# One activation on a column of ones, ahead of all other work on ScalarE

## The chip, the cores and the metric

The kernel runs on one NeuronCore of one Trainium2 chip. The time is that of one launch on the device in microseconds (us), and what counts is the median over several launches. The compute engines are TensorE (PE in the rows; PEld is its loading of weights), VectorE (DVE), ScalarE (ACT) and GpSimd (POOL). Most transfers are issued by the queue of the sync engine (SP). Each engine takes its own instructions in their written order and waits for the others through semaphores.

## The reference, cut to what matters

An attention with normalized queries and keys is followed by two feed-forward layers:

```
q_n, k_n = rmsnorm(q, g_q), rmsnorm(k, g_k)        # 4 batches, 12 heads, 448 rows, 64 columns, float32
attn = softmax(q_n @ k_n.T / sqrt(64)) @ v
x = attn, heads side by side                        # 1792 x 768
h = x @ w_in;  x = (h * sigmoid(1.702 * h)) @ w_out # 768 -> 2048 -> 768
h = x @ w_in2; out = (max(h, 0) + alpha * min(h, 0)) @ w_out2
```

## The kernel before

The work goes in pairs of heads. For each pair a tile `qk` (128 partitions, 2 x 7 x 64 float32) takes the rows of k and q by four transfers, and ScalarE squares it in two halves (function `normalize`, line 421, `sq<-qk`). VectorE adds up each half over 64 columns (line 423, `ss<-sq`), and GpSimd turns the sums of both halves into reciprocal roots by three rounds of Newton's method (lines 424 to 434, `ss`, `rs`, `tn`). VectorE then scales the rows (line 458, `qn<-qk,rs`), TensorE transposes them (lines 465 and 467, `qt`), and ScalarE copies the result out and multiplies it by a column of the gains (line 468, scale `g_col`). From there on scores, softmax and the product with v follow for each pair, while the weights of the first feed-forward layer are loaded and split into high and low halves (`w1i`, `w1o`). The three other batches of the attention run beside the first layer on TensorE, and the second layer is last: a product with `w2i`, a store of its result `g_dram`, and an output product (line 1090) whose operands `w2lo`, `w2hi`, `even` and `odd` are sums and differences of blocks.

The order on each engine is fixed when the program is built: a scheduler goes through the code and lays out one list of instructions for each engine. At the front of the program the code reads:

```
if True:
    make_identity(nc, ident)
    nc.vector.memset(ones, 1.0)
    nc.vector.tensor_copy(out=identf, in_=ident)
    load_qk(0)
    gains()
...
    next(w1i_steps)
    normalize(0)
```

`load_qk(0)` puts four transfers on the queue of SP (lines 378 to 381). `gains()` puts two more behind them, for `gq` and `gk`, the two gain vectors (lines 282 and 283); VectorE multiplies them (line 284, `gq<-gq,gk`) and makes the scaled tile `gs` from them (line 293), TensorE transposes it (line 296, `gt`), and ScalarE writes `g_col` (line 297). ScalarE has a table of functions that an instruction of its own, ACT_TABLE_LOAD, loads; no line of the code asks for it, the build puts it ahead of the first activation. In the whole program there is one, and all activations use the same table.

Of the kernel before, what the change touches and what calls it, by code (L numbers as in the profile page):

```python
# [9 lines left out]
F32 = mybir.dt.float32  # L10
# [3 lines left out]
AF = mybir.ActivationFunctionType  # L14
# [43 lines left out]
def attention_moe_kernel(  # L58
# [17 lines left out]
    nc = tc.nc  # L76
# [14 lines left out]
    small = ctx.enter_context(tc.tile_pool(name="small", bufs=2))  # L91
# [7 lines left out]
    ones = const.tile([128, 128], BF16, name="ones")  # L99
# [155 lines left out]
    def later_rows(w, d, other):  # L255

        nj = w.shape[1]
        return lambda j: w[:, j + d].rearrange("p e n -> p (e n)").bitcast(F32) if j + d < nj else other(j)
# [20 lines left out]
    def gains():  # L279
        gq = small.tile([128, D], F32, tag="gq", name="gq", bufs=1)  # L280
        gk = small.tile([128, D], F32, tag="gk", name="gk", bufs=1)
        nc.sync.dma_start(out=gq, in_=g_q.partition_broadcast(128))
        nc.sync.dma_start(out=gk, in_=g_k.partition_broadcast(128))
        nc.vector.tensor_tensor(out=gq, in0=gq, in1=gk, op=ALU.mult)
        gm = small.tile([128, 1], F32, tag="gm", name="gm", bufs=1)
        gi = small.tile([128, 1], F32, tag="gi", name="gi", bufs=1)
        nc.vector.tensor_reduce(out=gm, in_=gq, op=ALU.max, axis=AX, apply_absolute_value=True)
        pow2floor(c_s, gm)
        scaled_reciprocal(gi, c_s, 0.5)
        nc.vector.memset(gs[64:128, 3], 1.0)  # L290
        for c in range(4):
            ps = slice(0, 64 if c == 3 else 128)
            nc.vector.tensor_scalar(out=gs[ps, c], in0=gq[ps], scalar1=gi[ps], scalar2=None, op0=ALU.mult)
        nc.vector.tensor_scalar(out=c_s, in0=c_s, scalar1=2.0 ** -22, scalar2=None, op0=ALU.mult)
        gt = ps_m.tile([128, 128], F32, tag="m", name="gt")
        nc.tensor.transpose(out=gt, in_=gs[:, 0:2].rearrange("p c d -> p (c d)"), identity=identf)
        nc.scalar.activation(out=g_col, in_=gt[:, 0:1], func=AF.Copy, scale=c_s)

    def v_scales(b, col):
        one = small.tile([128, 1], F32, tag="vone", name="vone")  # L300
        nc.vector.tensor_reduce(out=one, in_=col, op=ALU.max, axis=AX)
        pow2floor(one, one)
        partition_max(mv[:, b:b + 1], one)
        scaled_reciprocal(av[:, b:b + 1], mv[:, b:b + 1], 2.0 ** 13)
# [65 lines left out]
    def load_qk(P):  # L370

        if P >= B * NP:
            return
        b, p = divmod(P, NP)
        qk = raw_p.tile([128, 2, NT2, D], F32, tag="qk", name="qk", bufs=QKB)
        places = qk.rearrange("p h c d -> p h (c d)")
        queue = loader(P)
        queue.dma_start(out=places[:, :, 0:3 * D], in_=main_rows(k, b, p))
        queue.dma_start(out=places[:, :, 4 * D:], in_=main_rows(q, b, p))
        queue.dma_start(out=qk[0:64, :, 3], in_=some_rows(k, b, p, ST))  # L380
        queue.dma_start(out=qk[64:128, :, 3], in_=some_rows(q, b, p, ST))
        raws[P] = qk

    def load_v(P):
        if P >= B * NP:
            return
        b, p = divmod(P, NP)
        if b:
            vr = raw_p.tile([128, 2, NV, D], F32, tag="vr", name="vr")
        else:  # L390
            firsts[P] = first_tiles(P)
            vr = firsts[P][1]
        queue = loader(P)
        queue.dma_start(out=vr.rearrange("p h c d -> p h (c d)")[:, :, 0:3 * D], in_=main_rows(v, b, p))
        h = 0 if b else 64
        queue.dma_start(out=vr[h:h + 64, :, 3], in_=some_rows(v, b, p, ST))
        queue.dma_start(out=vr[64 - h:128 - h, :, 3], in_=some_rows(v, b, p, 0, 3))
        rawv[P] = vr
# [783 lines left out]
    if True:  # L1182
        make_identity(nc, ident)
        nc.vector.memset(ones, 1.0)
        nc.vector.tensor_copy(out=identf, in_=ident)
        load_qk(0)
        gains()
        load_v(0)
        load_qk(1)
        load_v(1)  # L1190
        g0 = big.tile([128, KF, 2, S], F16, tag="g", name="g0")
        stage = g0.rearrange("p m e t -> p (m e t)").bitcast(F32)
        parts = stage[:, 0:R1I * 1024].bitcast(I32).rearrange("p (i n t) -> p i n t", i=R1I, t=2)
        raw1o = g0.rearrange("p m e t -> p m (e t)").bitcast(I32)[:, KF - 4 * R1O:, FIRST:].rearrange("p m (n t) -> p m n t", t=2)

        def num1i(j):
            if j == KD - 1:
                return stage[:, 5120:5120 + FF]
            return held.bitcast(F32)[:, (j - 3) * FF:(j - 2) * FF]

        def num1o(j):
            if j == KF - 2:
                return att_p.tile([128, 2 * NT2 * D], F32, tag="ph", name="num1o", bufs=PHB)[:, 0:DM]
            return raw_p.tile([128, 2 * NT2 * D], F32, tag="qk", name="num1o", bufs=QKB)[:, 0:DM]

        w1i_steps = weights(
            moe_w_in, "w1i", lambda: w1i, later_rows(w1i, 3, num1i), lambda t: parts[:, t % R1I], 4, R1I, 2.0 ** -14, scales,
            G1I
        )
        w1o_steps = weights(  # L1210
            moe_w_out, "w1o", lambda: w1o, later_rows(w1o, 2, num1o), lambda t: raw1o[:, 4 * (t % R1O):4 * (t % R1O) + 4], 2,
            R1O, 2.0 ** -25, scales, G1O
        )
        next(w1i_steps)
        normalize(0)
        for _ in prep_pair(0):
            pass
        for P in range(2, 1 + QKB):
            load_qk(P)
        load_v(2)  # L1220
        normalize(1)
        early = measure(1, B - 1, 4)
        for i, _ in enumerate(first_pairs()):
            if i >= 6:
                for _ in range(1):
                    next(early, None)
            for _ in range(W_RATE):
                next(w1i_steps, None)
        for _ in w1i_steps:
            pass  # L1230
        v_scales(0, v0)
        first_x()
        moe1_scales(0)
        for P in range(NP, NP + 2):
            load_qk(P)
            load_v(P)
        n1o = 0
        steps = attention([4 * P + r for P in range(NP) for r in range(2, 4)])
        for i, _ in enumerate(steps):
            pairs = max(0, (i - LAG + 1) // 2)  # L1240
            rows = KF - 2 if pairs >= 4 else (HOLD + pairs * HELD) // (2 * DM) - 2
            while n1o < min(1 + 2 * rows + 3 * (rows // 2), (i + 1) * W1O_RATE, 57):
                next(w1o_steps)
                n1o += 1
            if i >= M_AT and i - M_AT < KF:
                first_in(slice(0, FIRST), i - M_AT, g0)
            for _ in range(2):
                next(early, None)
        while n1o < 57:
            next(w1o_steps)  # L1250
            n1o += 1
        for m in range(len(range(2 * NP + LAG)) - M_AT, KF):
            first_in(slice(0, FIRST), m, g0)
        with tc.issue_after(loads["w1o"][W1O_HOLD].ins):
            normalize(NP, NP + 1)
            for _ in prep_pair(NP):
                pass
            load_qk(NP + 2)
            load_qk(NP + 3)
            load_v(NP + 2)  # L1260
        att_steps = other_batches()
        done = 4 * NP
        late = late_weights(ctx, att)
        for b in range(B):
            last = min(NU, 4 * NP * (b + 2)) + LAG2
            first = done
            got = None
            for i, _ in enumerate(moe1(b) if b else first_moe1(g0)):
                lead = 0 if b else B1_AT
                want = first + (last - first) * min(1.0, max(0.0, i + 1 - lead) / (PACE[b] * TICKS - lead))  # L1270
                while done < min(want, NU + LAG2):
                    next(att_steps)
                    done += 1
                if b == B - 1:
                    for _ in range(1 if i < 2 * KF else 2):
                        if got is None or i >= 2 * KF:
                            got = next(late, None)
        second_layer(late)
# [30 lines left out]
```

## Time and profile before

| what | us |
|---|---|
| median of 3 runs | 1150.96 |
| lowest and highest run | 1147.56, 1157.47 |
| time of the profiled execution | 1150.36 |
| its span, from the first to the last instruction | 1148.6 |

The profile is of one execution. Its time is 1.76 us more than its span. In that execution TensorE worked in 93% of the span and ScalarE in 60%, and TensorE's granted clock was 0.977 of full speed in the mean.

### The profile page before, as it was taken

The numbers are of one execution on the slowest core, as the hardware profiler recorded it, in microseconds if no ns is written. First come the engines' busy times: TensorE is split into PE (matmuls) and PEld (weight loads), VectorE is DVE, ScalarE is ACT, GpSimd is POOL, SyncE is SP. The second block draws the span as 40 slices with busy tenths as digits, with TensorE's granted clock in tenths as the row PEclk, the third lists the DMA queues.
The fourth block names the chain that finished last, engine by engine and source line by source line (L and its number), as shares of the span: only waits on it lengthen the run. The fifth ranks groups of instructions, "written<-read, shape, count | busy, mean of one in ns | idle before, by whom it ended". The sixth has DMA issues, their size and how long they took to land.

```text
span 1148.6 us, 18408 instructions
## 1 busy us (share of the span) xinstructions
PE 1069.4 (93%) x6753; PEld 585.0 (51%) x6753; DVE 802.1 (70%) x1397; ACT 693.2 (60%) x1452; POOL 179.4 (16%) x364
## 2 busy tenths in 40 slices
PE   4776889898989999999999999999999999999998
PEld 2343457744444445555455455444444477666664
DVE  5979798887879885577534865599976224959341
ACT  4778686888879876688633562356456425756120
POOL 2701003676433342100000000000000000000000
PEclk9978899899999999999999999999999999999999
DMA  7974743478888756455446501765351423363111
GB/s 227 258 178 132 182 129 109 97 158 184 183 191 167 160 130 151 109 121 118 78 124 229 203 1 64 249 215 194 136 171 59 138 70 113 106 184 101 33 31 28
DMA packets 235562, 158.19 MB, mean 138 GB/s; under 512 B 167888, under 2 KB 214736, under 8 KB 235472
## 3 DMA queue, kind: packets, MB, share of 16 engines
q1 hardware_dynamic: 229200, 141.34, 44.6%
q0 software_dynamic: 6272, 15.67, 5.3%
q8 instruction: 53, 0.87, 0.3%
q14 instruction: 37, 0.30, 0.1%
HBM read 92.35 MB, written 25.69 MB: 103 GB/s over the span
## 4 chain that ended last, share of the span: by engine, by line
PE 56%; DVE 16%; DMA 11%; issue 7%; ACT 6%; POOL 4%; SPq 1%; DVEq 0%; POOLq 0%; ACTq 0%
PE op L1090 17%; PE yp L821 15%; PE h L927 9%; PE hp L798 7%; PE xp L648 3%; PE sp L525 2%; DMA t<-hl 2%; PE hp L758 2%; DMA g<-in_moe_w_in_dram 2%; DVE nm L530 1%; DMA g<-in_moe_w_out_dram 1%; DVE g L141 1%; ACT pr L550 1%; DMA qk<-in_q_dram 1%; DMA yr<-y_dram 1%
## 5 line engine op out<-in xcount | busy, mean ns | idle before, releaser
L821 PE MATMUL yp<-g,w1o 128*128 128x448 f16 x1152 | 226.9, 354 | 1.5 <-DVE g L767 0.9
L927 PE MATMUL h<-x,w2i 128*128 128x512 f16 (+1 forms) x1152 | 219.3, 352 | 4.3 <-DVE pos L933 2.8
L798 PE MATMUL hp<-x,w1i 128*128 128x448 f16 x864 | 170.3, 353 | 1.6 <-DVE t L807 1.6
L927 PEld LDWEIGHTS <-w2i 128*128 128x128 f16 x1152 | 112.6, 98 | 109.6 <-issue 5.1
L821 PEld LDWEIGHTS <-w1o 128*128 128x128 f16 x1152 | 109.5, 98 | 110.8 <-issue 12.0
L798 PEld LDWEIGHTS <-w1i 128*128 128x128 f16 x864 | 81.9, 98 | 83.5 <-issue 9.6
L620 DVE SCALAR_TENSOR_TENSOR ph<-pr,sm,ph 128x448 f16<-128x448 f32 x126 | 85.2, 707 | 25.4 <-ACT ph L593 25.4
L530 DVE TENSOR_REDUCE nm<-sp 128x2 f32<-128x896 f32 x96 | 92.5, 964 | 10.3 <-PE sp L525 7.6
L932 ACT ACTIVATE pos<-h,sign 128x512 f32<-128x512 f32 (+1 forms) x64 | 40.1, 628 | 89.7 <-PE h L927 83.3
L550 ACT ACTIVATE pr<-sp,nm,c_s 128x448 f32<-128x448 f32 x126 | 89.9, 717 | 2.4 <-DVE ph L620 1.1
L1090 PEld LDWEIGHTS <-even 128*128 128x128 f16 x672 | 65.7, 98 | 43.5
L933 DVE SCALAR_TENSOR_TENSOR pos<-h,slope,pos 128x512 f32<-128x512 f32 (+1 forms) x64 | 43.4, 680 | 59.9 <-ACT pos L932 59.7
L593 ACT ACTIVATE ph<-pr,sm 128x448 f16<-128x448 f32 x126 | 77.6, 659 | 10.7 <-DVE sm L590 10.6
L758 PE MATMUL hp<-x,w1i 128*128 128x256 f16 (+1 forms) x576 | 66.1, 276 | 9.2 <-DVE g L767 5.2
L1090 PEld LDWEIGHTS <-odd 128*128 128x128 f16 x504 | 49.3, 98 | 32.6
L758 PEld LDWEIGHTS <-w1i 128*128 128x128 f16 x576 | 55.2, 104 | 20.2 <-issue 14.8
L1090 PE MATMUL op<-w2lo,even 128*128 128x384 f16 x384 | 63.5, 326 | 0.0
L648 PE MATMUL xp<-pt,vs 128*64 128x256 f16 (+1 forms) x792 | 49.8, 267 | 7.5 <-DMA pt<-ph 6.2
L525 PE MATMUL sp<-t 64*128 64x448 f16 (+1 forms) x432 | 54.0, 357 | 0.6 <-DMA t<-hl 0.5
L648 PEld LDWEIGHTS <-vs 128*64 128x64 f16 x792 | 37.9, 112 | 27.6 <-issue 17.2
L532 ACT ACTIVATE nm<-nm,c_s 128x2 f32<-128x2 f32 x72 | 20.9, 290 | 48.5 <-DVE nm L530 48.1
L1090 PE MATMUL op<-w2hi,even 128*128 128x384 f16 x288 | 47.5, 326 | 0.0
(243 smaller groups left out, 1659.7 us busy)
## 6 DMA issues: line engine op xcount, KB each, us to landing
g<-in_moe_w_in_dram SPq DMA_DIRECT2D x24, 512.0 KB, 6.1
g<-in_moe_w_out_dram SPq DMA_DIRECT2D x32, 384.0 KB, 4.0
w2raw<-in_moe_w_in_dram SPq DMA_DIRECT2D x24, 512.0 KB, 5.7
w2raw<-in_moe_w_out_dram SPq DMA_DIRECT2D x16, 768.0 KB, 6.4
g_dram<-pos SPq DMA_DIRECT2D x48, 256.0 KB, 2.0
gp<-g_dram SPq DMA_DIRECT2D x8, 1024.0 KB, 6.8
odd<-g_dram SPq DMA_DIRECT2D x6, 1024.0 KB, 5.5
y_dram<-y SPq DMA_DIRECT2D x24, 224.0 KB, 2.5
```

The costliest lines, as they stand in the source:

```text
L525: nc.tensor.matmul(out=sp[:, j, 0:S] if n == 2 else sp[ds, 0, 0:S], lhsT=qt[ds] if n == 2 else qt[ds, 64:128], rhs=kt[ds, 0:S], start=(i = ...
L530: nc.vector.tensor_reduce(out=nm[:, 0:n], in_=sp[:, 0:n, 0:S], op=ALU.max, axis=AX, negate=True)
L550: last = nc.scalar.activation(out=pr[i], in_=sp[:, i, 0:S], func=AF.Exp, bias=nm[:, i:i + 1], scale=c_s if u >= 4 * NP else 1.0, accum_out ...
L593: nc.scalar.activation(out=ph[:, i, 0:S], in_=pr[i], func=AF.Copy, scale=sm[:, i:i + 1])
L620: nc.vector.scalar_tensor_tensor(out=ph[:, i, S:2 * S], in0=pr[i], scalar=sm[:, i:i + 1], in1=ph[:, i, 0:S], op0=ALU.mult, op1=ALU.subtract)
L648: nc.tensor.matmul(out=xp[64 * j:64 * j + 64, t:t + n], lhsT=vs[ks, j, c], rhs=pt[ks, 7 * j + kc, 0:n] if b else pt[ks, kc, o:o + n], star ...
L758: nc.tensor.matmul(out=ps, lhsT=w1i[:, kk, e, m * 128:(m + 1) * 128], rhs=xs[0, kk][:, f, cols], start=(i == 0), stop=(i == 3 * KD - 1))
L798: nc.tensor.matmul(out=ps, lhsT=w1i[:, kk, e, m * 128:(m + 1) * 128], rhs=x[:, f], start=(n == 0), stop=(n == 3 * KD - 1))
L821: nc.tensor.matmul(out=ps, lhsT=w1o[:, m, e, j * 128:(j + 1) * 128], rhs=g[:, m, f], start=(n == 0), stop=(n == 3 * KF - 1))
L927: nc.tensor.matmul(out=ps, lhsT=w2i[:, kk, e, m * 128:(m + 1) * 128], rhs=x2[kk][:, f], start=(c == 0), stop=(c == 3 * KD - 1))
L933: nc.vector.scalar_tensor_tensor(out=pos, in0=ps, scalar=slope[:, m:m + 1], in1=pos, op0=ALU.mult, op1=ALU.max)
L1090: nc.tensor.matmul(out=ps, lhsT=ops[:, o, m, f], rhs=rhs[:, e], start=(c == 0), stop=(c == 3 * KH - 1))
```

## The change

One tile `first` of one column is taken from the pool `small`, and one activation writes the square of a column of ones into it. Nothing reads the tile.

```
@@ -1182,6 +1182,8 @@
     if True:
         make_identity(nc, ident)
         nc.vector.memset(ones, 1.0)
+        first = small.tile([128, 1], F32, tag="first", name="first", bufs=1)
+        nc.scalar.activation(out=first, in_=ones[:, 0:1], func=AF.Square)
         nc.vector.tensor_copy(out=identf, in_=ident)
         load_qk(0)
         gains()
```

On ScalarE, at the very front of the program, the load of the table had stood ahead of the first square and had waited with it for the transfers of `qk`. DMAHW0 to DMAHW7 are the semaphores of SP's transfers, in turn, and the numbers behind semaphores and buffers mean nothing here:

```order
-L1304 UNCONDITIONAL_BRANCH [waits barrier_Pool_Activation_PE_DVE_SP_release]
-L421 ACT_TABLE_LOAD [waits DMAHW2_49,DMAHW3_49,DMAHW1_49]
-L421 ACTIVATE sq<-qk 128x448 [waits DMAHW0_49]
+L1306 UNCONDITIONAL_BRANCH [waits barrier_Pool_Activation_PE_DVE_SP_release]
+L1186 ACT_TABLE_LOAD
+L1186 ACTIVATE first<-ones 128x1 [waits DVE_49]
+L421 ACTIVATE sq<-qk 128x448 [waits DMAHW2_49,DMAHW3_49,DMAHW1_49,DMAHW0_49]
 L421 ACTIVATE sq<-qk 128x448
 L297 ACTIVATE g_col<-gt,c_s 128x1 [waits PE_49]
```

The load now waits for nothing but the barrier at the start, the new activation waits for VectorE's memset of `ones`, and the first square waits for its four transfers by itself. On VectorE, at the same place, the list is as it was but for line numbers; DMAHW4 and DMAHW5 are the transfers of `gq` and `gk`:

```order
-L1304 UNCONDITIONAL_BRANCH [waits barrier_Pool_Activation_PE_DVE_SP_release]
+L1306 UNCONDITIONAL_BRANCH [waits barrier_Pool_Activation_PE_DVE_SP_release]
 L1184 MEMSET ones 128x128
 L290 MEMSET gs 64x64
-L1185 CAST identf<-ident 128x128 [waits Pool_49]
+L1187 CAST identf<-ident 128x128 [waits Pool_49]
 L423 TENSOR_REDUCE ss<-sq 128x7 [waits Activation_49]
 L284 TENSOR_TENSOR gq<-gq,gk 128x64 [waits DMAHW5_49,DMAHW4_49]
```

Nothing moved there: the product of the gains stands between the sum of the first half (the row above it) and the sum of the second half (the next row of the list, `L423` again). The lists of TensorE, GpSimd and SP are the same as before too, and all later rows of ScalarE and VectorE.

The new tile takes 4 bytes of each partition, for which the build sets aside 32. Every tile behind it in the on-chip memory therefore starts 32 bytes further on: 993 of the 1107 tiles, among them `qk`, `sq`, `hl`, `t`, `pt`, `vs`, `gp`, `w2hi`, `y` and `pos`. The large buffers for weights, `g`, `odd`, `even` and the second layer's `w2lo` keep their places. Before, nearly all the large moved tiles started at a multiple of 64 bytes, and now they start 32 past one; the unmoved ones start 32 past a multiple of 64 in both programs.

## Rows read from the trace of the kernel before

**Rows 1.** The page: engines' busy time; the chain that ended last, by engine and line.

```profile
PE 1069.4 (93%) x6753; PEld 585.0 (51%) x6753; DVE 802.1 (70%) x1397; ACT 693.2 (60%) x1452; POOL 179.4 (16%) x364
...
PE 56%; DVE 16%; DMA 11%; issue 7%; ACT 6%; POOL 4%; SPq 1%; DVEq 0%; POOLq 0%; ACTq 0%
PE op L1090 17%; PE yp L821 15%; PE h L927 9%; PE hp L798 7%; PE xp L648 3%; PE sp L525 2%; DMA t<-hl 2%; PE hp L758 2%; DMA g<-in_moe_w_in_dram 2%; DVE nm L530 1%; DMA g<-in_moe_w_out_dram 1%; DVE g L141 1%; ACT pr L550 1%; DMA qk<-in_q_dram 1%; DMA yr<-y_dram 1%
```

**Rows 2.** Timeline of ScalarE: start, length, instruction [idle before, what ended it].

```profile
4.79 1.28 ACT L421 ACT_TABLE_LOAD   x1 [4.79 <-DMA qk<-in_q_dram]
6.09 1.04 ACT L421 ACTIVATE sq<-qk 128x448 f32<-128x448 f32 x2
11.81 0.26 ACT L297 ACTIVATE g_col<-gt,c_s 128x1 f32<-128x1 f32 x1 [4.68 <-PE gt L296]
```

**Rows 3.** Timeline of VectorE, the first 10 us.

```profile
0.83 0.17 DVE L1184 MEMSET ones<- 128x128 bf16 x1 [0.83 <-PEq L1293]
...
6.70 0.62 DVE L423 TENSOR_REDUCE ss<-sq 128x7 f32<-128x448 f32 x1 [5.13 <-ACT sq L421]
8.60 0.23 DVE L284 TENSOR_TENSOR gq<-gq,gk 128x64 f32<-128x64 f32 x1 [1.28 <-DMA gk<-in_g_k_dram]
8.74 0.61 DVE L423 TENSOR_REDUCE ss<-sq 128x7 f32<-128x448 f32 x1
```

**Rows 4.** The chain that ended last, in order of time: start, length, link.

```profile
2.55 0.61 SPq L381
...
3.21 0.59 SPq L282
...
3.84 4.65 DMA gk<-in_g_k_dram
...
8.60 0.23 DVE gq L284
8.82 0.54 DVE ss L423
...
9.45 0.27 POOL ss L424
...
13.34 0.23 POOL rs L434
...
13.59 0.07 DVE qn L458
```

**Rows 5.** Groups of instructions, shapes apart: count, busy us, mean ns, idle before.

```profile
L1090 PE MATMUL op<-w2lo,even 128*128 128x384 f16 x384 | 63.5, 326 | 0.0
L1090 PE MATMUL op<-w2hi,even 128*128 128x384 f16 x288 | 47.5, 326 | 0.0
...
L1030 ACT ACTIVATE gp<-gp,cg 128x256 f32<-128x256 f32 x64 | 26.4, 494 | 12.8 <-DMA gp<-g_dram 8.3 <-DVE cg L1163 4.5
...
L1030 ACT ACTIVATE odd<-odd,cg 128x256 f32<-128x256 f32 x48 | 19.7, 496 | 10.9 <-DMA odd<-g_dram 10.9
...
L165 DVE SCALAR_TENSOR_TENSOR w2n<-w2raw,w2n 128x512 int32<-128x512 int32 x24 | 15.8, 685 | 0.1
...
L165 DVE SCALAR_TENSOR_TENSOR w1i<-g,w1i 128x512 int32<-128x512 int32 x12 | 8.1, 684 | 0.1
```

**Rows 6.** DMA issues by line: count, KB each, median us from issue to landing.

```profile
g<-in_moe_w_in_dram SPq DMA_DIRECT2D x24, 512.0 KB, 6.1
...
w2raw<-in_moe_w_in_dram SPq DMA_DIRECT2D x24, 512.0 KB, 5.7
...
gp<-g_dram SPq DMA_DIRECT2D x8, 1024.0 KB, 6.8
odd<-g_dram SPq DMA_DIRECT2D x6, 1024.0 KB, 5.5
y_dram<-y SPq DMA_DIRECT2D x24, 224.0 KB, 2.5
```

**Rows 7.** All transfers into the tile `gp`.

```profile
DMA to landing us min/median/max: 5.1/6.8/9.1
```

**Rows 8.** All transfers into the tile `odd`.

```profile
DMA to landing us min/median/max: 5.2/5.5/7.8
```

More of the change, by code (lines that the diff above doesn't have):

```diff
@@ L1184, in attention_moe_kernel @@
         nc.vector.memset(ones, 1.0)
+        first = small.tile([128, 1], F32, tag="first", name="first", bufs=1)
+        nc.scalar.activation(out=first, in_=ones[:, 0:1], func=AF.Square)
         nc.vector.tensor_copy(out=identf, in_=ident)
```

## The prediction

> **What bounds the kernel now.** I read the page first. Its chain that ended last is 56% TensorE, and ScalarE holds 6% of it, DMA 11% [rows 1]. TensorE is busy in 93% of the span and ScalarE in 60%, so an instruction on ScalarE is worth its length only where nothing else is late beside it. The instruction that moves lies in the first 14 us, and there TensorE's share says nothing: the stretch is one chain of small steps, and the question is which step is last at each join. So the next views are the timelines of ScalarE and VectorE, and then the chain in order of time.
>
> On ScalarE the table load starts at 4.79 us, when the last transfer of `qk` that it waits for has landed, and takes 1.28 us [rows 2]. The two squares start 0.02 us behind it and end at 6.09 + 1.04 = 7.13 us. The first of them releases VectorE's sum at 6.70 [rows 3], and on that view alone the load seems to cost 1.28 us: VectorE sat idle 5.13 us until then. But the next row of VectorE is the product of the gains, which waited another 1.28 us for the transfer of `gk` and began at 8.60. (That the load and this wait are both 1.28 us long is chance.) The sum of the second half stands behind that product and began at 8.74, 1.61 us after its own input was ready at 7.13. GpSimd needs both sums, and started at 9.45 [rows 4].
>
> The chain in order of time says the same from the other side. It begins with SP's issues, goes into the transfer of `gk` (issued at 3.84, 4.65 us long), and from its landing into the gains at 8.60, the second sum at 8.82, GpSimd at 9.45 to 13.57 and the scaling of the rows at 13.59 [rows 4]. Neither the load nor the squares are links of it. The start of this kernel is bound by the sixth transfer in SP's queue.
>
> **The change part by part.** *The load leaves its place.* The first square can start where the load started, at 4.79, and both end at 4.79 + 1.04 = 5.83 us instead of 7.13. The first sum then starts about 6.70 - 1.30 = 5.40 and ends at 6.02. Behind it VectorE meets the product of the gains, as before, and the order of VectorE and SP is unchanged, so the transfer of `gk` is issued and lands when it did. The wait there grows from 1.28 to 8.60 - 6.02 = 2.58 us. The second sum starts at 8.74 as before. What is late next is thus not a new thing but the one that was late already: the saving of 1.30 us is turned into wait on VectorE. The two squares of the second pair cannot use it either, since the copy to `g_col` at 11.81 stands ahead of them on ScalarE [rows 2], and it hangs on the gains too. On the path: 0.
>
> *The load at its new place.* It waits only for the barrier at the start, behind which VectorE's first instruction ran at 0.83 [rows 3]. I take the same for ScalarE: an estimate of 0.83 to 2.11 us, in a stretch where ScalarE did nothing for 4.79 us. The cover is 2.7 us up to the landing of `qk` at 4.79, and from there another 2.8, since the two squares are late for the gains only if they start after 8.60 - 1.04 = 7.56. Without the cover it would cost its 1.28 us, which it did not even at its old place. So 0.
>
> *The new activation.* The nearest row is the other activation of one column, `g_col`, 0.26 us [rows 2]. Its input, the memset of `ones`, ends at 0.83 + 0.17 = 1.00, before the load ends, so it waits for nothing of its own: about 2.11 to 2.4 us, under the same cover. Queued behind it on ScalarE is only the first square, which waits for `qk` to 4.79. Nobody waits for `first`. Cost 0; without cover 0.26.
>
> *The 32 bytes.* Every tile behind the new one starts 32 bytes later. For the compute engines the trace before has both alignments side by side, since `w2lo` sat 32 past a multiple of 64 and `w2hi` on one: 326 ns for a matmul with either [rows 5]. ScalarE took 494 ns on `gp` (on a multiple) and 496 on `odd` (32 past one), VectorE 685 and 684 for the same operation on `w2n` and `w1i`. So 0 for the engines. For transfers the rows are further off, because load differs between stages: `odd`, 32 past, landed in 5.5 us in the median against 6.8 for `gp`; `g`, 32 past, in 6.1 against 5.7 for `w2raw` [rows 6]. The two pairs have opposite signs, and the least disturbed transfers of the first pair differ by 0.1 us, 5.1 against 5.2 [rows 7, 8]. I take 0 and keep, for the range, 0.1 / 5.1 = 2% either way, and 6.1 / 5.7 = 7% as an upper bound; I leave out the 1.3 us by which the median of `odd` is better, because the minimum shows none of it. On the chain DMA has 11%, of which 3% are the loads of `g`, which does not move [rows 1]: 8% of 1148.6 = 92 us. So -1.8 to +6.4 us, and 0 taken.
>
> The sum is 0 + 0 + 0 + 0: the profiled execution's 1150.36 us stays. The median of the runs shown is 0.6 us above it, with runs from 1147.56 to 1157.47, so the forecast for the median is **1151.0 us**. A difference of under 1%, 11.5 us, is about what a measurement of this kernel cannot tell from no change.
>
> **The rivals.** *A: the load was on the path.* Then 1.28 us come off, 1151.0 - 1.3 = 1149.7 us. For it speaks that ScalarE and VectorE both stood still for the load; against it the second sum, which was ready 1.61 us before it ran, and the chain, which goes through `gk`. It would take a `gk` that lands 1.6 us earlier than in this trace before the squares count at all, and 2.9 us earlier for the whole price. By the Trainium skill, page "ScalarE: Activation LUTs", section "What ACT_TABLE_LOAD costs", a load takes about 1283 ns and a drain of about 1380 ns with it, 2.66 us in all; by that this rival would give an estimated 1148.3 us. The trace agrees with the 1283 ns and shows no drain: the square starts 0.02 us behind the load [rows 2]. Here the engine had nothing in flight to drain.
>
> *B: the shift slows the transfers.* This is the case on the slower side. The transfers of `hl` to `t`, of `ph` to `pt`, of `y`, of `gp` and of `qk` all read or write moved tiles, and they make 8% of the chain. At 2% more they cost 1.8 us, at 7% more 6.4 us: 1152.8 to 1157.4 us. It would be over 1% only where these transfers got 11.5 / 92 = 12.5% longer. Against it stand the equal minima of `gp` and `odd` [rows 7, 8]; for it, that the transposes have no row at the other alignment, so nothing here excludes that they mind. The Trainium skill says in "DMA: Bandwidth & Descriptors", section "How a descriptor splits into AXI transactions", that a transfer is cut at multiples of 256 bytes of address and that a descriptor which does not start on one also fetches the bytes from the boundary down to its start, in beats of 32 bytes. That speaks against this change: a row of `y` of 1792 bytes went from 128 past such a boundary to 160 past it, 60 beats to 61, an estimated 1.7% more. By that the 92 us would grow by an estimated 1.6 us. No run so far shows it; the minima of `gp` and `odd` neither exclude nor need it.
>
> *C: the change doesn't do what it says.* The load could take longer at the front than at its old place, or be repeated. The order has one load, at the front, so the second is out. For the first, the load may last up to 7.56 - 0.26 - 0.83 = 6.5 us, five times its 1.28, before the gains wait for a square; past that the time grows one for one: at ten times its length it would be 12.8 - 6.5 = 6.3 us, 1157.3.
>
> **How the numbers follow.** The forecast, no change beyond the scatter of the runs, has 0.74. A has 0.08, B 0.14, C 0.02, and 0.02 are left for what I don't see. The range goes down to the lowest run shown less the 1.8 us by which transfers may get better, 1145.8, and up to 1157.5, which is the upper end of B and the highest run shown alike. The forecast, A, most of B and C lie in it; what is left out is the far end of B and a median of the new runs outside the runs of before, together some 2 in 10. Faster by over 1% would need 11 us that no row offers: 0.02. Slower by over 1% is B beyond 12.5%: 0.04. The rest, 0.94, is within 1%.
>
> **What would show it.** In the changed kernel's trace the load should begin near 0.8 us and last 1.28, the activation on `ones` follow it at 0.3 us or less, and the first square begin near 4.8. The first sum on VectorE should come at about 5.4 with some 3.8 us idle before it, and the product of the gains at about 8.6 with 2.6 us idle before it instead of 1.28, still released by `gk`. The second sum, GpSimd's first step (9.45) and the row scaling (13.59) should stand within some 0.2 us of where they stood. The matmul groups should keep 326 ns, and the medians of `gp` and `y` their 6.8 and 2.5 us. I am wrong in the start if the second sum runs by the squares and not by the gains, and wrong in the rest if the transfers on moved tiles, the transposes above all, land later by more than a few per cent while those into `g` do not.

## The result, and the profile after

The changed kernel takes 1158.77 us in the median of 22 runs (1151.67 to 1165.62), the kernel before 1150.57 us in 22 runs. The ratio is 1.0068, with a 95% interval of 1.005 to 1.0087: slower by 7.8 us (5.8 to 10.0) on 1150.57; the two medians lie 8.2 us apart. It was forecast unchanged, at 1151.0 us. Ratios and intervals in this document leave out three single executions far off all others: 1393.27 us of the kernel before, 2178.43 us of the shift by 128 bytes, and 2755.26 us of the kernel with only the transposes' sources moved, which was its profiled one.

The page of the changed kernel, engines and the chain that ended last, against [rows 1]:

```profile
PE 1069.4 (92%) x6753; PEld 583.9 (50%) x6753; DVE 804.7 (69%) x1397; ACT 693.6 (60%) x1453; POOL 181.6 (16%) x364
...
PE 52%; DMA 15%; DVE 14%; issue 7%; ACT 6%; POOL 4%; SPq 1%; DVEq 0%; ACTq 0%; POOLq 0%
```

TensorE and ScalarE have the same work to the microsecond, VectorE and GpSimd 2.6 and 2.2 us more, and the span is 10.1 us longer, 1158.7 after 1148.6. The chain says where to look: DMA's share of it went from 11% to 15%, and TensorE's fell.

The front of the program is the first place to check. The timeline of ScalarE, against [rows 2]:

```profile
0.72 1.28 ACT L1186 ACT_TABLE_LOAD   x1 [0.72 <-PEq L1295]
2.02 0.20 ACT L1186 ACTIVATE first<-ones 128x1 f32<-128x1 bf16 x1
4.76 1.04 ACT L421 ACTIVATE sq<-qk 128x448 f32<-128x448 f32 x2 [2.54 <-DMA qk<-in_q_dram]
12.18 0.26 ACT L297 ACTIVATE g_col<-gt,c_s 128x1 f32<-128x1 f32 x1 [6.38 <-PE gt L296]
```

And that of VectorE, against [rows 3]:

```profile
0.82 0.17 DVE L1184 MEMSET ones<- 128x128 bf16 x1 [0.82 <-PEq L1295]
...
5.37 0.62 DVE L423 TENSOR_REDUCE ss<-sq 128x7 f32<-128x448 f32 x1 [3.81 <-ACT sq L421]
8.97 0.23 DVE L284 TENSOR_TENSOR gq<-gq,gk 128x64 f32<-128x64 f32 x1 [2.98 <-DMA gk<-in_g_k_dram]
9.11 0.61 DVE L423 TENSOR_REDUCE ss<-sq 128x7 f32<-128x448 f32 x1
```

The load runs at 0.72 us with nothing beside it, and the squares start 1.33 us earlier than before. All of that is turned into wait for `gk`: VectorE idles 2.98 us for it, where it had idled 1.28. The second sum follows the gains by 0.14 us, as before. In this execution `gk` landed 0.37 us later, so even this stretch ends later, but 0.4 us is not 10.

So where are the 10 us? The products of the attention with v (line 648, operands `pt` and `vs`) run through the three later batches and nowhere else; each row of the view by line gives the first and the last start. Before:

```profile
L648 PE MATMUL xp<-pt,vs x792: 246/272/370, 239.7 to 614.1; 128*64 128x256 f16 x108, 128*64 128x192 f16 x90
```

After:

```profile
L648 PE MATMUL xp<-pt,vs x792: 246/272/422, 240.5 to 625.7; 128*64 128x256 f16 x108, 128*64 128x192 f16 x90
```

The first product is 0.8 us late, the last 11.6. Behind it nothing more is lost; the first matmul of the second layer starts at 740.7 us instead of 729.5, 11.2 later, and the span ends 10.1 later. In this pair of executions the whole loss lies in the attention of the three later batches, which is the part with transposes by DMA. The view by stretches, from the first start of these products to the last (length; busy time and count of PE, PEld, DVE, ACT, POOL; TensorE's granted clock; DMA share; GB/s), before:

```profile
239.70:614.10 374.40, 365.65 (x2588) 183.81 (x2587) 257.10 (x436) 278.93 (x667) 106.41 (x202) 0.99 0.64 142
```

After:

```profile
240.50:625.70 385.20, 369.75 (x2588) 185.01 (x2587) 257.90 (x434) 278.14 (x663) 107.94 (x202) 0.98 0.71 138
```

Of the 10.8 us more, 6.7 are idle time of TensorE (15.45 us instead of 8.75), and 4.1 are longer busy time for the same 2588 matmuls, at a granted clock of 0.98 of full speed in the mean instead of 0.99. The DMA engines are busy in 71% of it instead of 64%. The largest wait of TensorE there is the one for `pt`, which the transposes write (us, times, longest), before:

```profile
PE xp L648 <- DMA pt<-ph: 6.2, 3, 3.2
```

After:

```profile
PE xp L648 <- DMA pt<-ph: 13.8, 5, 6.2
```

Operands that moved do not slow the engines, as the page's groups from the second layer show, against [rows 5]:

```profile
L1090 PE MATMUL op<-w2lo,even 128*128 128x384 f16 x384 | 63.5, 326 | 0.0
L1090 PE MATMUL op<-w2hi,even 128*128 128x384 f16 x288 | 47.5, 326 | 0.0
...
L1030 ACT ACTIVATE gp<-gp,cg 128x256 f32<-128x256 f32 x64 | 26.3, 495 | 11.9 <-DMA gp<-g_dram 8.4 <-DVE cg L1163 3.5
```

`w2hi` and `gp` moved by 32 bytes, and take 326 and 495 ns where they took 326 and 494. Some transfers do not keep their time. The issues in the changed kernel (count, KB each, median us to landing), the first four with rows of before in [rows 6]:

```profile
g<-in_moe_w_in_dram SPq DMA_DIRECT2D x24, 512.0 KB, 5.9
...
gp<-g_dram SPq DMA_DIRECT2D x8, 1024.0 KB, 6.8
odd<-g_dram SPq DMA_DIRECT2D x6, 1024.0 KB, 5.4
...
y_dram<-y SPq DMA_DIRECT2D x24, 224.0 KB, 2.4
...
vr<-in_v_dram POOLq DMA_DIRECT2D x16, 192.0 KB, 3.7
...
vs<-vs SPq DMA_DIRECT2D x36, 48.0 KB, 2.8
pt<-ph SPq DMA_TRANSPOSE x90, 4.1
...
t<-hl SPq DMA_TRANSPOSE x18, 4.4
```

The same view before, of the last four, for which the prediction gave no row:

```profile
vr<-in_v_dram POOLq DMA_DIRECT2D x16, 192.0 KB, 3.2
...
vs<-vs SPq DMA_DIRECT2D x36, 48.0 KB, 2.3
...
pt<-ph SPq DMA_TRANSPOSE x90, 3.6
...
t<-hl SPq DMA_TRANSPOSE x18, 3.7
```

The transposes take 19% (into `t`) and 14% (into `pt`) longer in the median, and the copies inside `vs` and the loads into `vr`, which run beside them, 22% and 16%. `gp` and `y`, moved as well, are as fast as before. The transposes into `pt` are of two sizes. The 54 that read 128 x 1792 numbers (line 627) and the 36 that read 64 x 896, a quarter of that (line 632), took before:

```profile
DMA to landing us min/median/max: 3.4/3.6/7.1
DMA to landing us min/median/max: 2.4/3.4/5.1
```

And after:

```profile
DMA to landing us min/median/max: 4.0/4.3/9.1
DMA to landing us min/median/max: 2.6/3.6/8.7
```

The large ones lose 0.6 us at their shortest, the small ones 0.2. The page's row of SP's transfers shows the same in sum, before:

```profile
q1 hardware_dynamic: 229200, 141.34, 44.6%
```

And after:

```profile
q1 hardware_dynamic: 229200, 141.34, 47.0%
```

Packets and megabytes are equal, but they held each of the 16 DMA engines for 47.0% of 1158.7 = 545 us instead of 44.6% of 1148.6 = 512. The single packets in the two traces tell whose time this is. The 149,504 packets of 256 bytes on this queue, of which the transposes make up an estimated 145,152 by the shapes of what they read, held each engine for 217.9 us instead of 186.1, and all its other packets for 326.2 instead of 326.6. So the added time is that of the transposes; the copies beside them land later, but hold the engines no longer.

### The profile page after: what moved, and what is told of

The parts are those of the page before. It is cut to its first block, busy times and chain, and to the rows that moved or that the text cites. A ratio compares the mean times of both kernels' runs of the same rounds, so it can differ in the third digit from the quotient of the medians.

```text
span 1158.7 us, 18409 instructions
## 1 busy us (share of the span) xinstructions
PE 1069.4 (92%) x6753; PEld 583.9 (50%) x6753; DVE 804.7 (69%) x1397; ACT 693.6 (60%) x1453; POOL 181.6 (16%) x364
## 4 chain that ended last, share of the span: by engine, by line
PE 52%; DMA 15%; DVE 14%; issue 7%; ACT 6%; POOL 4%; SPq 1%; DVEq 0%; ACTq 0%; POOLq 0%
PE op L1090 16%; PE yp L821 14%; PE h L927 9%; PE hp L798 7%; DMA qk<-in_q_dram 4%; PE xp L648 3%; DMA g<-in_moe_w_out_dram 2%; DMA g<-in_moe_w_in_dram 2%; PE sp L525 2%; ACT pr L550 1%; DMA pt<-ph 1%; DMA t<-hl 1%; DMA yr<-y_dram 1%; DVE g L141 1%; DVE w2num L165 1%
## 5 line engine op out<-in xcount | busy, mean ns | idle before, releaser
L821 PE MATMUL yp<-g,w1o 128*128 128x448 f16 x1152 | 229.4, 356 | 1.1 <-ACT g L140 0.7
L620 DVE SCALAR_TENSOR_TENSOR ph<-pr,sm,ph 128x448 f16<-128x448 f32 x126 | 87.7, 727 | 23.6 <-ACT ph L593 23.5
L593 ACT ACTIVATE ph<-pr,sm 128x448 f16<-128x448 f32 x126 | 77.6, 659 | 11.6 <-DVE sm L590 10.9
L758 PE MATMUL hp<-x,w1i 128*128 128x256 f16 (+1 forms) x576 | 63.3, 269 | 10.0 <-DVE g L767 6.3
```

Of the source, the lines that this page charges most:

```text
L593: nc.scalar.activation(out=ph[:, i, 0:S], in_=pr[i], func=AF.Copy, scale=sm[:, i:i + 1])
L620: nc.vector.scalar_tensor_tensor(out=ph[:, i, S:2 * S], in0=pr[i], scalar=sm[:, i:i + 1], in1=ph[:, i, 0:S], op0=ALU.mult, op1=ALU.subtract)
L758: nc.tensor.matmul(out=ps, lhsT=w1i[:, kk, e, m * 128:(m + 1) * 128], rhs=xs[0, kk][:, f, cols], start=(i == 0), stop=(i == 3 * KD - 1))
L821: nc.tensor.matmul(out=ps, lhsT=w1o[:, m, e, j * 128:(j + 1) * 128], rhs=g[:, m, f], start=(n == 0), stop=(n == 3 * KF - 1))
```

## The experiments

Theory 1: the shift by 32 bytes slows transfers on moved tiles. Theory 2, the rival: something of the load or the activation at the front costs. Five kernels tell them apart, two with one part of the change each and three with another size of the shift. Each ratio here is of 7 to 12 runs against 28 or 35 of the kernel before.

**The tile alone.** VectorE sets it, and the load stays where it was.

```
+        first = small.tile([128, 1], F32, tag="first", name="first", bufs=1)
+        nc.vector.memset(first, 1.0)
```

> The kernel before with the tile alone: first is taken from the pool, so that everything behind it moves by 32 bytes, and VectorE sets it instead of ScalarE; the table's load stays in front of the first square. Theory 1, the shift of 32 bytes slows the transfers on moved tiles: as slow as the changed kernel, 1.005 to 1.009 of before, transposes into t in the median near 4.4 us (3.7 before) and into pt near 4.1 (3.6). Theory 2, the load and the activation at the front are what costs: 1.000 within 0.002, transposes at 3.7 and 3.6.

Measured: 1.0063 (1.0041 to 1.0086), transposes into `t` at 4.5 us and into `pt` at 4.1. The tile alone, with no activation in front, gives the loss of the whole change within the intervals.

**The activation alone.** It writes into `g_col`, which the build has anyway.

```
+        nc.scalar.activation(out=g_col, in_=ones[:, 0:1], func=AF.Square)
```

> The activation on a column of ones stands in front, but writes into g_col, which is overwritten later, so that no tile moves. Theory 1 (the shift): 1.000 within 0.002 of before, with the first square at 4.8 us and the gains still the late step at 8.6 to 9.0. Theory 2 (the front): 1.005 to 1.009.

Measured: 0.9993 (0.9971 to 1.0015), transposes at 3.7 and 3.7. Theory 2 is out, and the load at the front is worth nothing that can be measured. The interval alone would still have room for the 1.3 us of rival A of the prediction (0.9989), but VectorE's timeline has not: the first sum comes 1.21 us earlier than before, `gk` landed early in this execution, and still the second sum follows the gains:

```profile
5.49 0.62 DVE L423 TENSOR_REDUCE ss<-sq 128x7 f32<-128x448 f32 x1 [3.94 <-ACT sq L421]
8.13 0.23 DVE L284 TENSOR_TENSOR gq<-gq,gk 128x64 f32<-128x64 f32 x1 [2.02 <-DMA gk<-in_g_k_dram]
8.28 0.61 DVE L423 TENSOR_REDUCE ss<-sq 128x7 f32<-128x448 f32 x1
```

**Other sizes of the shift.** The change, with a wider tile (16, 32 and 64 columns):

```
-        first = small.tile([128, 1], F32, tag="first", name="first", bufs=1)
-        nc.scalar.activation(out=first, in_=ones[:, 0:1], func=AF.Square)
+        first = small.tile([128, 16], F32, tag="first", name="first", bufs=1)
+        nc.scalar.activation(out=first[:, 0:1], in_=ones[:, 0:1], func=AF.Square)
```

By 64 bytes:

> The change with first made 64 bytes wide: all that the change moves is moved by 64 bytes. Theory 1 in the form that what counts is a start at a multiple of 64 bytes: 1.000 within 0.002 of before, transposes at 3.7 and 3.6 us. Theory 1 in the form of cuts at multiples of 256 bytes, by which any start off such a boundary costs: the tiles hl, t, pt and vs now start 64 past one, so transposes stay at 4.1 to 4.4 us and the time at 1.005 or more. Theory 2 (the front): 1.005 to 1.009.

By 256 bytes:

> The change with first made 256 bytes wide: every moved tile keeps its place with respect to boundaries of 256 bytes and of all smaller powers of two. Theory 1 in either form: 1.000 within 0.002 of before, transposes at 3.7 and 3.6 us. Theory 2 (the front): 1.005 to 1.009.

By 128 bytes:

> The change with first made 128 bytes wide, so that all moved tiles move by 128 bytes: hl, t, pt, vs and vr now start 128 past a multiple of 256, and qk, y, pos, gp, yr and ob, which had started 128 past one, on one. Boundaries of 256 count: transposes at 4.1 to 4.4 us, copies inside vs near 2.8, the loads of qk by GpSimd no longer than before (3.9) or shorter, the time 1.002 to 1.007. Boundaries of 128 count: transposes at 3.7 and 3.6, 1.000 within 0.002.

Measured: 64 bytes 1.0051 (1.0028 to 1.0073), 128 bytes 1.0038 (1.0011 to 1.0066), 256 bytes 0.9996 (0.9974 to 1.0017). A shift that keeps the place against multiples of 256 costs nothing, all others cost. The transfers that read `hl` are the clearest sign: their shortest is 3.4 us in every profile with `hl` on a multiple of 256 and 4.0 in every one with it off. The view by tile gave 3.4/3.7/6.6 us (shortest, median, longest) before. At 64 bytes:

```profile
DMA to landing us min/median/max: 4.0/4.5/6.4
```

At 128 bytes:

```profile
DMA to landing us min/median/max: 4.0/4.4/6.3
```

At 256 bytes:

```profile
DMA to landing us min/median/max: 3.4/3.7/6.7
```

At 32 bytes, in the changed kernel, it was 4.0/4.4/6.4. The step is the same 0.6 us for 32, 64 and 128, and a packet of 256 bytes took 23.3, 23.2 and 23.5 ns in the mean, 19.9 before. The shift by 128 also put `qk` on a multiple of 256, and GpSimd's loads of q did not get shorter for it (4.0 us, 3.9 before).

Next: which of the moved tiles is it? Pads in front of single tiles move them alone. The helper is the same in the four kernels that follow; each names its pads in bytes.

```
+    class Padded:
+        def __init__(self, pool, **pads):
+            self.pool, self.pads = pool, pads
+        def tile(self, shape, dtype, tag, **kw):
+            n = self.pads.pop(tag, 0)
+            if n:
+                self.pool.tile([128, n // 4], F32, tag="pad_" + tag, name="pad", bufs=1)
+            return self.pool.tile(shape, dtype, tag=tag, **kw)
```

**Only what the transposes read.**

```
+    att_p = Padded(att_p, hl=32, p=224, ph=32)
```

> The kernel before with pads in front of hl and ph, so that only the tiles that the transposes read start 32 bytes past a multiple of 256; qn and num1o, which share their places, move along, and all others keep their place with respect to 256. Theory S, transposes mind where they read: into t 4.4 us and into pt 4.1 in the median, the time near the changed kernel's, 1.004 to 1.008. Theory T, they mind where they write: 3.7 and 3.6, 1.000 within 0.002. Theory V, not the transposes but the loads into vr and qk and the copies inside vs make up the loss: 1.000 within 0.002 as well, with vs at 2.2.

Measured: 1.0048 (1.0024 to 1.0072). Its profile is of the execution of 2755.26 us and is not read, so the same kernel was measured once more:

> The same kernel as in the run with only the sources of the transposes moved, once more, because its profiled execution was disturbed. Theory S: 1.003 to 1.007 of before, transposes into t at 4.4 us and into pt at 4.1, copies inside vs near 2.8 although vs has not moved, because they stand behind transposes in the queue. If these copies stay at 2.3, their delay in the changed kernel is of vs itself.

Measured: 1.0059 (1.0034 to 1.0084), near the whole loss, with an issue view that looks like the changed kernel's:

```profile
vr<-in_v_dram POOLq DMA_DIRECT2D x16, 192.0 KB, 3.7
...
vs<-vs SPq DMA_DIRECT2D x36, 48.0 KB, 2.7
pt<-ph SPq DMA_TRANSPOSE x90, 4.1
...
t<-hl SPq DMA_TRANSPOSE x18, 4.5
```

`vr` and `vs` stand at their old places here, and are late all the same.

**Only what the transposes write**, with `vs` between them.

```
+    att_p = Padded(att_p, pt=32, ph=224)
```

> The kernel before with pads in front of pt and ph, so that the tiles into which the transposes write (pt and t1, named t in the rows) and vs between them start 32 bytes past a multiple of 256, and hl, ph and all others keep their place. Theory S: transposes at 3.7 and 3.6 us, and only the copies inside vs longer (2.8 instead of 2.3), the time 1.000 to 1.003. Theory T: transposes at 4.4 and 4.1, the time 1.004 to 1.008. Theory V: transposes unchanged, copies inside vs at 2.8, the time 1.002 to 1.008.

Measured: 0.9984 (0.9958 to 1.001). All four groups are as before:

```profile
vr<-in_v_dram POOLq DMA_DIRECT2D x16, 192.0 KB, 3.6
...
vs<-vs SPq DMA_DIRECT2D x36, 48.0 KB, 2.3
pt<-ph SPq DMA_TRANSPOSE x90, 3.6
...
t<-hl SPq DMA_TRANSPOSE x18, 3.6
```

(`vr`, not moved, at 3.6 shows how far that one scatters, so its 3.7 above is no proof of a delay.) Theories T and V are out. The copies inside `vs` are slow with an unmoved `vs` when transposes read off a multiple of 256, and fast with a moved `vs` when they don't.

**Of the sources, `ph` alone.**

```
+    att_p = Padded(att_p, ph=32)
```

> The kernel before with ph alone 32 bytes past a multiple of 256 (the source of the 90 transposes of the probabilities), hl where it was. Theory S, by count of bytes: ph is the source of 54 large and 36 small transposes, hl of 18 large ones, so most of the loss is here: 1.003 to 1.006, pt at 4.1 us, t at 3.7 or a little above. If the 18 transposes into t are what the chain waits for: under 1.002.

Measured: 1.0049 (1.0021 to 1.0078), `pt` at 4.1 us. `t` came to 4.0 in the median though `hl` had not moved and its shortest stayed 3.4: the transposes of the probabilities carry most of the loss, and the transposes into `t` get slower beside them. `hl` alone was not moved, so its own part is not measured.

**The change, with the sources put back.**

```
+    att_p = Padded(att_p, hl=224)
```

> The changed kernel with a pad of 224 bytes in front of hl, so that hl, ph and the tiles between and behind them start at a multiple of 256 again; all other tiles that the change moved (qk, vr, vst, sq, y, pos, gp, yr, ob, w2hi) stay moved by 32 bytes. Theory S, the sources of the transposes are nearly all of the loss: 1.000 within 0.002 of before, transposes at 3.7 and 3.6 us. If the other moved tiles cost too: 1.002 to 1.005 with transposes at 3.7 and 3.6.

`vs` and the targets `pt` and `t`, which lie between, go back with them. Measured: 1.0017 (0.9996 to 1.0037), transposes at 3.7 and 3.7, SP's transfers at 44.7% of the engines. This undoes most of the loss with the early load and the activation still in. Whether the other moved tiles cost the last 0.2% is within the interval and stays open.

**Every large tile on a multiple of 256**, to see if the kernel before left something too: a pad of 160 bytes in `small`, one of 128 in front of `vr`, and two one-column tiles put into one, by which `g`, `odd`, `even` and the weights come to a multiple.

```
+    small.tile([128, 40], F32, tag="pad", name="pad", bufs=1)
+    raw_p = Padded(raw_p, vr=128)
-        co = const.tile([128, 1], F32, name=f"co{i}")
+        if i < 3:
+            w2["co"] = const.tile([128, 2], F32, name=f"co{i}")
+        co = w2["co"][:, i // 3:i // 3 + 1]
```

> The kernel before with every large tile at a multiple of 256 bytes, by two pads and one small tile fewer; hl, t, pt, vs and vr were there already, and qk, y, pos, gp, yr, ob (128 past) and the big buffers g, odd and w (32 past) now are. If boundaries of 256 count for all transfers: loads of qk from 3.9 to about 3.6, loads into g a little shorter, the time 0.995 to 1.000. If only transposes and copies from the memory on the chip mind: 1.000 within 0.002.

Measured: 0.9978 (0.995 to 1.0005). With the early activation into `g_col` added:

> The kernel with every large tile at a multiple of 256 bytes, and the early activation in front, written into g_col so that it moves nothing. If the alignment of all tiles is worth something and the activation nothing: 0.995 to 0.999 of before, as without the activation (0.998). If that first value was scatter: 1.000 within 0.002.

Measured: 0.998 (0.9952 to 1.0008). Both beat the changed kernel clearly and the kernel before not clearly: each interval reaches 1. The early activation adds nothing that can be measured here either. In the first of the two, the tiles `gp` and `odd`, whose loads the prediction compared, stand on a multiple of 256; the shortest load takes what it took at 128 past one (`gp`, 5.1 us) and at 32 past (`odd`, 5.2). `gp` and `odd` there:

```profile
DMA to landing us min/median/max: 5.1/6.7/8.7
DMA to landing us min/median/max: 5.1/5.6/7.5
```

**All profiles together.** Seven profiles have `ph` on a multiple of 256 (before, the activation alone, the shift by 256, the targets alone, the sources put back, and the two with every large tile on a multiple), six have it off (the change, the tile alone, the shifts by 64 and 128, the sources alone measured again, and `ph` alone). In each of these rows the two groups do not overlap:

| | on (7) | off (6) |
|---|---|---|
| products with v, first start to last, us | 374.4 to 380.3 | 382.9 to 385.2 |
| TensorE idle in that stretch, us | 8.75 to 14.45 | 15.45 to 17.03 |
| DMA share in that stretch | 0.63 to 0.65 | 0.69 to 0.72 |
| packets of 256 bytes, us on each DMA engine | 183.5 to 193.4 | 211.2 to 219.8 |
| copies inside `vs`, median us | 2.1 to 2.3 | 2.7 to 2.8 |

The wait for `pt` scatters more, 6.2 to 11.4 us against 10.6 to 14.5. The profile of before has the shortest stretch and the shortest wait of its group, so the 10.8 us between the pair shown first are at the wide end of what the change costs there.

## Why the prediction was wrong

**The start was right.** The saving at the squares became wait for `gk`, VectorE's first sum came at 5.37 us (forecast 5.40), its wait for the gains grew to 2.98 us (forecast 2.58, with a `gk` 0.37 us later), and the activation alone measured 0.9993. The second sum came 0.37 us late with that `gk`, more than the 0.2 us that was allowed for. The load's new place (0.72 us, forecast 0.83) and the activation (0.20 us, forecast 0.26) cost nothing that can be measured, by the cover that was named.

**The engines were right.** Operands at either alignment take the same time, 326 ns and 495 ns, as rows of before had shown.

**The step that failed is the term of the 32 bytes for transfers**, "I take 0", with 1.8 and 6.4 us as its ends. It measured 7.8 us for the change, 7.3 for the tile alone (0.63% of the 1151.88 us of its runs of before). Two things were wrong in it. The rows it rested on were loads that write into a tile (`odd`, `gp`, `g`, `w2raw`), and such loads indeed do not mind, as the kernel with every large tile on a multiple showed for `gp` and `odd`. But of the pair with equal minima `odd` started 32 past a multiple of 256 and `gp` 128 past one: neither stood on the boundary that turned out to count, so the pair could not speak of it for any transfer. What minds is a transpose that reads from the tile, and of these the prediction itself said that they had no row at the other alignment. Loads were then let stand for them, and the 7% that bounded the term came from loads too, where the transposes got 14 and 19% longer.

**Rival B was the right one, with a chance of 0.14**, and its mechanism was right in the place and too wide in its tiles: not all transfers on moved tiles, only the reads of `hl` and `ph` by the transposes. Its price by shares of the chain, 92 us times a per cent, is not how the time came about. Those 92 us are all of the chain's DMA but `g`, and of the moved tiles [rows 1] name only `t<-hl`, `qk` and `yr`, 4% together. The transposes into `t` had 2% of that chain, those into `pt` too little for a place among its first fifteen; yet `ph` alone cost 0.49%. What the traces show in its place: the transposes' packets hold each DMA engine 32 us longer, and the stretch of the products with v gets longer, with more idle time of TensorE in it. The chain after names the loads of q (1% before, 4% after), but that share is no steady sign, since it is 1% with `ph` alone too. How the copies inside `vs` are delayed, behind the transposes in SP's queue or beside them on the engines, is not shown.

**The skill's rule had the right boundary.** Shifts of 32, 64 and 128 bytes cost and one of 256 does not. The Trainium skill says, in "DMA: Bandwidth & Descriptors", section "How a descriptor splits into AXI transactions", that a transaction has to start on a multiple of 256 bytes, and that a descriptor which starts elsewhere also pays for the bytes below its start. The runs agree with that boundary for transposes. By the page's count of beats a start 32 past would cost one beat and a start 128 past four; here the shortest transfer from `hl` took 4.0 us at 32, 64 and 128 alike. By its count of transactions, 256 bytes that start on the boundary are one and off it two, at each of these distances, and the transposes' packets are of 256 bytes; the equal step fits that, but that it is the cause is not shown. For ordinary stores the prediction's estimate of 1.7% for `y` would be 0.04 us of 2.5, and that row scatters from 2.4 to 2.8 us over the thirteen profiles, so the runs do not decide it.

**The range** ended at 1157.5, the upper end of B, and the time came out 1.3 us past it. Of the chances, "within 1%" held, in part by luck: it rested on B's transfers staying under 12.5% more, and the transposes got more than that, while `gp` and `y` got none. And a difference under 1% was not beyond measurement, as the prediction had it; with 22 runs of each kernel the interval is 0.2% to either side.

## What to carry to other kernels

A small tile added ahead of others is also a shift of everything behind it, and must be costed as that: list which tiles change their place against 256 bytes, and which transfers read them. Tiles that a DMA transpose reads belong on a multiple of 256 bytes here. And a load hidden under a wait for something else gains nothing by being moved; the instruction next to the wait in the list, not the one that released the first step, says what is late.

## What the hardware showed that I had not expected

A transpose by DMA takes longer when its source starts off a multiple of 256 bytes, and the distance does not matter: 0.6 us on 3.4 for the shortest into `t`, at 32, 64 and 128. The step is not fixed, but smaller for a smaller transpose: 0.6 us on 3.4 for the large ones into `pt`, and 0.1 to 0.2 on 2.4 for those with a quarter of the bytes. The target's place does not matter (3.6 us at 32 past, 3.7 on a multiple). The copies inside `vs`, which share the time with such transposes, land later without being moved themselves, 2.7 us instead of 2.3.
